# Attention and a mixture of experts in one kernel: the weight loads of experts 0, 1 and 2 are issued at other places

## The chip, the cores and the metric

The kernel runs on one core of a Trainium2 chip. The metric is the device time of one execution in microseconds (us). The core has five engines that work side by side, each through its own list of instructions in a fixed order: PE (TensorE, matrix products), ACT (ScalarE), DVE (VectorE), POOL (GpSimd) and SP (SyncE). They wait for one another, and for data transfers (DMAs), through semaphores. A DMA is issued by an engine, lands later, and its landing is what others wait for.

## The reference

Block-causal attention over 8 batches, 8 heads, 576 positions and 64 dimensions, and then a layer of 8 experts over its 4608 tokens of width 512; every token is given to two of the experts.

```python
# attention: q, k, v are 8 x 8 x 576 x 64
scores = scale * np.matmul(q, k.transpose(0, 1, 3, 2))
block_i = pos[:, None] // 64
block_j = pos[None, :] // 64
scores = np.where(block_i >= block_j, scores, -1000000000.0)
scores = scores - np.max(scores, axis=-1, keepdims=True)
attn = np.exp(scores)
attn = attn / (np.sum(attn, axis=-1, keepdims=True) + 1e-09)
attn_out = np.matmul(attn, v)

# experts: x is 4608 x 512, w1 is 8 x 512 x 1024, w2 is 8 x 1024 x 512
logits = x @ w_gate
noisy_logits = logits + np.log1p(np.exp(x @ w_noise)) * noise
top2 = np.argpartition(-noisy_logits, 2, axis=1)[:, :2]
# top2_w: softmax over the two chosen logits
for e in range(E):
    for k in range(2):
        mask = top2[:, k] == e
        h = np.maximum(x[mask] @ w1[e], 0.0)
        out[mask] += top2_w[mask, k, None] * (h @ w2[e])
```

## The kernel before

**Attention.** The batches are worked through in four groups of two (g = 0 to 3). A group has 26 score slots, two half groups of 13, and the slots are counted through: slot u = 26 g + place, 0 to 103. In every slot the main loop issues one score unit: PE's score matmuls (L297, L308) into the PSUM tile `sc`, and ACT's exponential of it into `esc` (L300, and L311 in the last slot of a half group). Behind the score unit come the steps that the program has put at that slot with `at(slot, function, arguments)`; `run(slot)` issues them, in an order of rank where several stand at one slot. The loads of weights and the scatters have the last rank, and among themselves the order in which they were put. The whole order of every engine is thus written out by hand: nothing is reordered later, and what an engine does waits for what stands before it in its own list.

The steps of a group g, apart from its score units:

- `load_all` (L206) brings raw q and k of group g+2, `load_v` (L210) the v tiles `vt` of group g+1, 16 small loads each. `transpose_qk` (L254) turns raw q and k on PE.
- `av_tile` (L339, L350) multiplies the exponentials by v; DVE divides by the sum (L354 for the reciprocal, L355 for the product) and writes the result as rows of `xr`, one tile of tokens after another. At a group's first tile POOL clears and fills some columns of the new `xr` (L327, L328). There are three `xr` buffers, so that group 3's waits for the scatters of group 0.
- `x_transpose` (L369, L370) and `router` (L382 to L469: PE, ACT and DVE in small steps) choose each token's two experts and its row in their lists.
- `scatter` (L489) writes rows of `xr` to a buffer in DRAM, `xd`, ordered by expert. It is an indirect DMA that POOL issues, 18 per group, with the row numbers from the router. It waits for an exponential of one or two slots before.

The scatters of group 0 stand at slots 52 to 69, of group 1 at 78 to 95, of group 2 at 101 to 114 and of group 3 at 118 to 131. Slots from 104 on have no score unit; from 111 on every slot is a step of the experts.

**Experts.** Groups 0 and 1 are one half of the tokens, groups 2 and 3 the other. For each half and expert, in the order (0,0), (0,1), (0,2), (1,0), (1,1), (1,2), (0,3), (1,3) and on, `load_x` brings that expert's rows, transposed, from `xd` (SP, L509, `xa` for the first and `xg` for the others; the first waits for all scatters of its half); `layer1` (L564 on PE, L567 on ACT) has eight steps and `layer2` (L576 on PE, L581 on ACT, L586 on DVE) five. Results of a token's first expert go to DRAM (`yd`, L583), are gathered for its second (L604, POOL), and the sum is scattered to the output (L588, POOL).

**Weights.** `load_w(pool, e, k)` (its DMA is L230) brings a quarter of expert e's weights: k = 0 and 1 are halves of `w1sb`, k = 2 and 3 halves of `w2sb`, 512 KB each in the buffer. The source is float32 and the buffer bfloat16; the DMA converts, and POOL issues it. Pool `wE` has room for two experts, 0 and 1. Pool `wM`, for expert 2, is opened at slot 91, when the raw q and k are no longer used. Later experts come during the expert steps.

**POOL's queue** therefore holds, in one order: raw q and k, v, weights, scatters, gathers and the output's scatters. A DMA that POOL issues waits for the eighth one before it on that queue to have landed, since eight semaphores are used in turn.

In the lines below `UG` is 26.

Of the kernel before, what the change touches and what calls it, by code (L numbers as in the profile page):

```python
# [19 lines left out]
def kernel(  # L20
# [43 lines left out]
    UG = 2 * UN  # L64
# [32 lines left out]
    wE = main.enter_context(tc.tile_pool(name="wE", bufs=2))  # L97
# [524 lines left out]
    def at(slot, fn, *args):  # L622
        todo.setdefault(slot, []).append((fn, args))

    def run(slot):

        def rank(item):
            fn, args = item
            if fn is router_step:
                return 3 if rgen_n.get(args[0], 0) in (0, 1, 2, 8, 14, 15) else 0  # L630
            return {av_tile: 1, transpose_qk: 2, x_transpose: 2}.get(fn, 4)

        items = todo.pop(slot, [])
        while items:
            items.sort(key=rank)
            fn, args = items.pop(0)
            fn(*args)
# [131 lines left out]
    at(UG + 4, clear_x, 0, UG + 3)  # L769
    at(2 * UG + 4, clear_x, 1, 2 * UG + 3)  # L770
    for k in range(4):
        at(UG + 1 + 2 * k, load_w, wE, 0, k)
        at(2 * UG - 6 + k, load_w, wE, 1, k)
    for u in range(NG * UG):
        score_unit(*divmod(u, UG))
        run(u)
        if u == 3 * UG + 13:
            raws_up.close()
            ffn["x"] = raws_up.enter_context(tc.tile_pool(name="xgp", bufs=3, side="right", reuse_waits="tile"))
            ffn["rec"] = raws_up.enter_context(tc.tile_pool(name="recp", bufs=1, side="right", reuse_waits="tile"))  # L780
            wM = raws_up.enter_context(tc.tile_pool(name="wM", bufs=1, side="right", reuse_waits="tile"))
            at(3 * UG + 18, load_x, 0)
            at(3 * UG + 19, load_x, 1)
            at(3 * UG + 20, load_rec, 0)
            at(3 * UG + 21, load_x, 2)
            for k in range(4):
                at(4 * UG + 12 + 3 * k, load_w, wM, 2, k)

    WL = {}

# [141 lines left out]
```

## Time and profile before

| | us |
|---|---|
| seven runs, sorted | 489.25, 490.5, 492.11, 496.56, 496.75, 497.06, 497.95 |
| their median | 496.56 |
| the profiled run's own time | 489.71 |
| its span (first to last instruction) | 487.8 |

Every time that follows is of that one profiled execution, in us from the start of its span. The busy times of the page, as shares of the span:

| engine | busy us | share |
|---|---|---|
| PE | 413.0 | 85% |
| ACT | 253.7 | 52% |
| POOL | 245.9 | 50% |
| DVE | 162.4 | 33% |

The span falls into these parts, by the last exponential of each half group and the first and last matmul of the experts:

| part | from | to |
|---|---|---|
| groups 0 and 1 (slots 0 to 51) | 0 | 75 |
| group 2, first half (slots 52 to 64) | 75 | 92 |
| group 2, second half (65 to 77) | 92 | 114 |
| group 3, first half (78 to 90) | 114 | 132 |
| group 3, second half (91 to 103) | 132 | 167 |
| rest of group 3, its transposes and router (104 to 110) | 167 | 194 |
| matmuls of the experts | 194 | 448 |
| last gathers and scatters of the output | 448 | 488 |

On POOL, the loads of expert 0 are issued at 46.1 to 49, those of expert 1 at 80.5 to 90.7, those of expert 2 at 201.5 to 219.3. The first scatter of group 0 is issued at 92.75, the last of group 1 at 154.78; those of group 2 run from 166.3 to 183.9, those of group 3 from 196.7 to 231.9.

How to read a line of the profile. A line of the timeline has the start, the duration, the engine and the source line, the operation, what it writes and reads, and in brackets the idle time of that engine before it, with what ended it: another engine's instruction, a DMA, "issue" when the engine waited for nothing that the profile shows, "remote" when a semaphore that no instruction in the trace explains came last. "PEclk" is the clock that was granted to PE, as a share of the full one. "DMA share" is the sum over queues of the time that packets took, as a share of the core's 16 DMA engines; since packets of one engine overlap, it can pass 1. The chain of waits is followed back from the last instruction: at each step to what released it.

### The profile page before, as it was taken

The page shows a single profiled execution, that of the slowest core. Times are in us where ns is not written, and L with a number is a line of the kernel's source. Part 1 is how long each engine was busy: PE and PEld are TensorE (multiplying, and loading weights), DVE is VectorE, ACT ScalarE, POOL GpSimd, SP SyncE. Part 2 cuts the span into 40 slices and gives each one's busy share as a digit, 9 for nine tenths or more (in the row PEclk, how much of TensorE's full clock was granted, in tenths as well). Part 3 has the DMA queues.
Part 4 walks back from the last instruction along what each step waited for, and adds up shares of the span by engine and source line. Part 5 has one row for each costly group of instructions (what it writes and reads, how often), then busy time and mean ns, then how long its engine had stood idle before and what let it go on. Part 6 is the DMA issues. An engine that isn't in the chain of part 4 may idle for free.

```text
span 487.8 us, 9833 instructions
## 1 busy us (share of the span) xinstructions
PE 413.0 (85%) x3952; PEld 255.0 (52%) x3952; DVE 162.4 (33%) x508; ACT 253.7 (52%) x343; POOL 245.9 (50%) x293
## 2 busy tenths in 40 slices
PE   3889879878930717997999999999989999999994
PEld 2456556655620416653655655665555664565562
DVE  1677678666640704820030011011011112113112
ACT  2999878866830500553545544554544554554340
POOL 8778225248876270587240123353537465565533
PEclk9989988975965755998999999999999999999998
DMA  9999999997932940488998668798899999864222
GB/s 143 158 142 177 229 208 182 223 232 106 119 112 89 159 146 24 99 183 212 136 222 179 97 154 184 131 213 194 141 225 198 183 237 240 168 187 166 76 80 97
DMA packets 134569, 78.67 MB, mean 161 GB/s; under 512 B 95937, under 2 KB 124355, under 8 KB 134516
## 3 DMA queue, kind: packets, MB, share of 16 engines
q0 software_dynamic: 70304, 55.78, 69.0%
q1 hardware_dynamic: 54132, 13.00, 15.1%
q10 hardware_dynamic: 10080, 9.18, 5.8%
q8 instruction: 33, 0.54, 0.5%
q14 instruction: 20, 0.16, 0.1%
HBM read 68.28 MB, written 33.13 MB: 208 GB/s over the span
## 4 chain that ended last, share of the span: by engine, by line
PE 66%; DMA 8%; ACT 6%; issue 6%; another core or an unknown queue 6%; DVE 3%; POOL 3%; POOLq 0%; DVEq 0%
PE yp L576 24%; PE hp L564 23%; PE av L339 6%; DMA raw<-in_k_dram 5%; PE sc L297 5%; ACT esc L300 4%; PE tp L254 3%; PE av L350 2%; PE tp L369 2%; POOL out_dram L588 2%; DMA yg<-yd,orow 1%; DMA yd<-ysb 1%; ACT hq L267 1%; DVE xr L355 1%
## 5 line engine op out<-in xcount | busy, mean ns | idle before, releaser
L576 PE MATMUL yp<-w2sb,hq 128*128 128x512 bf16 x640 | 142.7, 382 | 4.3 <-issue 2.6
L564 PE MATMUL hp<-xg,w1sb 128*128 128x320 bf16 x960 | 133.7, 299 | 1.9 <-ACT hq L567 1.3
L564 PEld LDWEIGHTS <-w1sb 128*128 128x128 bf16 x1024 | 100.1, 98 | 44.1 <-issue 3.1
L567 ACT ACTIVATE hq<-hp 128x640 bf16<-128x640 f32 x128 | 89.7, 703 | 60.3 <-PE hp L564 53.7
L586 DVE SCALAR_TENSOR_TENSOR yo<-yp,wrow,yg 128x512 f32<-128x512 f32 x46 | 34.5, 751 | 234.3 <-ACT ysb L581 183.2
L300 ACT ACTIVATE esc<-sc 128x1024 bf16<-128x1024 f32 x96 | 94.7, 1026 | 32.6 <-remote 18.9
L576 PEld LDWEIGHTS <-hq 128*128 128x128 bf16 x640 | 63.0, 98 | 78.8 <-issue 7.1
L489 POOL DMA_INDIRECT xd<-xr,slots x72 | 70.7, 982 | 55.4 <-issue 14.3
L604 POOL DMA_INDIRECT yg<-yd,orow x46 | 47.4, 1031 | 86.2 <-ACT hq L567 62.6
L581 ACT ACTIVATE ysb<-yp,wrow 128x512 bf16<-128x512 f32 x70 | 48.1, 687 | 79.9 <-PE yp L576 64.1
L588 POOL DMA_INDIRECT out_dram<-yo,trow x46 | 45.7, 994 | 58.1 <-DVE yo L586 48.1
L339 PE MATMUL av<-vt,esc 128*128 128x65 bf16 x640 | 35.6, 213 | 32.8 <-DVE xr L355 16.2
L339 PEld LDWEIGHTS <-esc 128*128 128x128 bf16 x640 | 27.8, 110 | 48.3 <-DVE xr L355 22.4
L297 PE MATMUL sc<-hq 64*128 64x512 bf16 (+4 forms) x320 | 42.5, 335 | 10.2 <-ACT esc L300 8.7
L210 POOL DMA_DIRECT2D vt<-in_v_dram x40 | 34.5, 875 | 20.1 <-DMA raw<-in_k_dram 5.6
L355 DVE TENSOR_TENSOR xr<-av,rden 128x256 bf16<-128x256 f32 x72 | 30.5, 424 | 2.7
L254 PE MATMUL tp<-ident,raw 128*64 128x128 bf16 x512 | 24.3, 247 | 6.7 <-DMA raw<-in_k_dram 3.7
L354 DVE RECIPROCAL rden<-av 128x4 f32<-128x4 f32 x72 | 13.3, 184 | 43.9 <-remote 28.7
L267 ACT ACTIVATE hq<-tp 128x1024 bf16<-128x1024 bf16 (+1 forms) x20 | 17.1, 853 | 16.3 <-PE tp L254 7.1
L254 PEld LDWEIGHTS <-raw 128*64 128x64 bf16 x512 | 18.6, 125 | 11.5 <-DMA raw<-in_k_dram 4.1
L297 PEld LDWEIGHTS <-hq 64*128 64x128 bf16 x320 | 12.4, 97 | 19.3 <-issue 11.4
L260 DVE COPY hq<-tp 128x1024 bf16<-128x1024 bf16 (+1 forms) x24 | 14.4, 598 | 8.8 <-PE tp L254 4.5
(122 smaller groups left out, 229.5 us busy)
## 6 DMA issues: line engine op xcount, KB each, us to landing
yd<-ysb ACTq DMA_DIRECT2D x70, 128.0 KB
w1sb<-in_moe_w_dram POOLq DMA_DIRECT2D x16, 512.0 KB
w2sb<-in_moe_w_dram POOLq DMA_DIRECT2D x16, 512.0 KB
vt<-in_v_dram POOLq DMA_DIRECT2D x32, 128.0 KB
raw<-in_q_dram POOLq DMA_DIRECT2D x2, 1152.0 KB
raw<-in_k_dram POOLq DMA_DIRECT2D x2, 1152.0 KB
xd<-zero SPq DMA_DIRECT2D x16, 132.0 KB
raw<-in_q_dram POOLq DMA_DIRECT2D x8, 256.0 KB
```

What stands on the lines that cost most here:

```text
L254: nc.tensor.transpose(to[64 * hf:64 * hf + 64, :, r, :], raw[:, (t0, t1)[hf], r * 64:(r + 1) * 64], ident)
L297: nc.tensor.matmul(out=sc[:, hf, off:off + z - a], lhsT=kT[sl, c0 + jt * P:c0 + jt * P + P], rhs=qT[sl, c0 + a:c0 + z], start=True, stop=True)
L300: ins = nc.scalar.activation(out=esc[:, hh, :, piece * 512:(piece + 1) * 512], in_=sc, func=AF.Exp, scale=scale)
L339: nc.tensor.matmul(out=av[:, hh, :], lhsT=esc[:, hh, hf, c:c + P], rhs=vb[:, 4 * hf + jt, h, :], start=(jt == 0), stop=(jt == ib))
L355: nc.vector.tensor_tensor(out=xr[:, idx, st * SET * D:(st + 1) * SET * D].rearrange("p (h d) -> p h d", h=SET), in0=av[:, :, 0:D], in1=rde ...
L489: ins = nc.gpsimd.indirect_dma_start(out=xd[half].bitcast(I32), out_offset=bass.IndirectOffsetOnAxis(ap=slots[:, g * TG + idx, i:i + 1], a ...
L564: nc.tensor.matmul(out=hp[:, n, 0:NW], lhsT=w1sb[:, db, fb * P:(fb + 1) * P], rhs=xgs[b][:, db, n * NW:(n + 1) * NW], start=(db == 0), sto ...
L567: ins = nc.scalar.activation(out=hs[b][:, fb, :].rearrange("p (n w) -> p n w", n=2), in_=hp[:, :, 0:NW], func=AF.Relu)
L576: nc.tensor.matmul(out=yp, lhsT=hs[b][:, fb, c * P:(c + 1) * P], rhs=w2sb[:, fb, :], start=(fb == 0), stop=(fb == FB - 1))
L581: ins = nc.scalar.activation(out=ysb, in_=yp, func=AF.Copy, scale=w)
L588: ins = nc.gpsimd.indirect_dma_start(out=out, out_offset=bass.IndirectOffsetOnAxis(ap=trow[half][:, e, c:c + 1], axis=0), in_=yo, in_offse ...
L604: ins = nc.gpsimd.indirect_dma_start(out=yg, out_offset=None, in_=yd[half][0:e * CAP, :], in_offset=bass.IndirectOffsetOnAxis(ap=orows[hal ...
```

## The change

Three numbers of slots change. Expert 0's four loads go from slots 27, 29, 31, 33 to 46, 47, 48, 49, where expert 1's were. Expert 1's go from there to slots 80, 84, 88, 92. Expert 2's go from slots 116, 119, 122, 125 to 112, 114, 117, 120.

```diff
     for k in range(4):
-        at(UG + 1 + 2 * k, load_w, wE, 0, k)
-        at(2 * UG - 6 + k, load_w, wE, 1, k)
+        at(2 * UG - 6 + k, load_w, wE, 0, k)
+        at(3 * UG + 2 + 4 * k, load_w, wE, 1, k)
     for u in range(NG * UG):
         score_unit(*divmod(u, UG))
         run(u)
@@
             for k in range(4):
-                at(4 * UG + 12 + 3 * k, load_w, wM, 2, k)
+                at(4 * UG + (8, 10, 13, 16)[k], load_w, wM, 2, k)
```

In POOL's queue this takes four loads out of the second group's stretch, puts expert 0's loads ahead of the first scatter of group 0, puts expert 1's among the scatters of group 1, one after the third, the seventh, the eleventh and the fifteenth, and lets the first load of expert 2 follow the fifteenth scatter of group 2. The other engines' orders are the same as before.

## The prediction

> **What bounds the kernel now.** I read the table of engine time by stretches first, cut at the ends of the half groups of 13 score slots (slot 65 begins near 92, 78 near 114, 91 near 132, 104 near 167).
>
> ```profile
> 75.00:92.00 17.00, 16.87 (x328) 12.15 (x329) 13.63 (x39) 13.48 (x16) 7.06 (x9) 0.90 1.76 207
> 92.00:114.00 22.00, 15.80 (x248) 10.27 (x248) 13.72 (x48) 15.21 (x22) 10.86 (x11) 0.74 0.99 199
> 114.00:132.00 18.00, 17.67 (x326) 12.42 (x326) 13.15 (x38) 13.27 (x16) 15.98 (x19) 0.85 1.11 120
> 132.00:167.00 35.00, 13.72 (x200) 8.41 (x198) 13.80 (x52) 13.69 (x20) 19.09 (x22) 0.61 0.51 113
> 167.00:194.00 27.00, 11.54 (x181) 9.71 (x182) 9.20 (x27) 0.67 (x2) 12.91 (x14) 0.57 0.40 97
> 194.00:448.00 254.00, 247.44 (x1487) 144.41 (x1485) 43.00 (x108) 127.65 (x188) 117.02 (x122) 0.99 0.83 178
> ```
>
> After the stretch and its length stand the busy times of PE, PE's weight loads, DVE, ACT and POOL, then PE's granted clock, DMA share and GB/s. From 194 on the experts keep PE at 247 of 254 us. The odd stretches are 132–167 and 167–194: no engine is busy for even 60% of them, and the DMA share is at its lowest. A half group elsewhere takes 17 to 22 us. The chain of waits names what ends last there:
>
> ```profile
> 45.13 19.55 DMA raw<-in_k_dram
> ...
> 141.96 10.70 another core or an unknown queue
> 153.32 5.22 another core or an unknown queue
> 169.72 2.38 another core or an unknown queue
> 172.77 7.87 another core or an unknown queue
> ```
>
> The timeline shows the middle of it:
>
> ```profile
> 151.83 0.21 POOL L328 COPY xr<-tokm 128x9 int32<-128x9 int32 x1
> 152.21 0.99 POOL L489 DMA_INDIRECT xd<-xr,slots  x1 [0.16 <-issue]
> 152.68 0.18 DVE L354 RECIPROCAL rden<-av 128x4 f32<-128x4 f32 x1 [10.72 <-remote]
> ...
> 154.78 0.97 POOL L489 DMA_INDIRECT xd<-xr,slots  x1 [0.30 <-issue]
> 157.61 1.02 ACT L300 ACTIVATE esc<-sc 128x1024 bf16<-128x1024 f32 x1 [13.82 <-remote]
> ```
>
> PE finished the av tile that L354 reads at 138.5 and the scores that L300 reads at 139.1, but its word of it reached DVE at 152.7 and ACT at 157.6; PE then stood for want of their buffers (10.3 us before 153.4, 5.5 before 159.3). All that time POOL issued the second group's scatters, each 0.97 us and 0.30 of issue, one directly behind the other. The word came just after two other instructions of POOL (L327, L328), and again after the last scatter (154.78). From 166.3 to 183.9 it repeats with the third group's 18 scatters (PE waits of 2.4, 8.1, 1.3 and 2.0). Where scatters alternate with v loads, 114–131, PE is busy 17.67 of 18. So I read 35 and 27 us as a half group of about 18 and a tail of about 14, drawn out by unbroken trains of scatters. What makes the signals late I cannot see.
>
> **The change part by part.** [...]No load is added.
>
> *Expert 0's four loads leave slots 27–33 for 46–49.* On POOL they cost 4 x 0.77 us (their own row). Behind them it is their transfers that count: they landed at 67.2, 69.6, 72.1 and 74.8, so 4 x 2.5 = 10 us of the queue, and the v loads behind waited for each:
>
> ```profile
> 59.37 0.87 POOL L210 DMA_DIRECT2D vt<-in_v_dram  x1 [5.00 <-DMA raw<-in_q_dram]
> 65.21 0.88 POOL L210 DMA_DIRECT2D vt<-in_v_dram  x1 [4.97 <-DMA raw<-in_k_dram]
> 67.43 0.87 POOL L210 DMA_DIRECT2D vt<-in_v_dram  x1 [1.34 <-DMA w1sb<-in_moe_w_dram]
> 69.88 0.88 POOL L210 DMA_DIRECT2D vt<-in_v_dram  x1 [1.58 <-DMA w1sb<-in_moe_w_dram]
> ...
> 92.75 1.09 POOL L489 DMA_INDIRECT xd<-xr,slots  x1 [1.36 <-DMA xd<-zero]
> ```
>
> Every transfer from POOL waits for the eighth before it. The raw q and k of the third group lie ahead of expert 0's loads, so PE's waits for them (1.55 us at 58.9, 2.56 at 64.7) stay: worth 0 here. What gains is POOL's backlog: expert 0's loads now take the place that expert 1's had, all behind comes some 10 us sooner, and the first group's scatters, placed at slots 52 to 69 (75 to 98) but begun at 92.75, can begin at about 82 and end near 120 instead of 131. PE's time hides all this (16.87 of 17 busy until 92), so by itself it gives 0; if the cover were gone, 10 us at most. Expert 0 is then in at about 95 and needed after 165.
>
> *Expert 1's loads leave 46–49 for 80, 84, 88, 92.* POOL's order for the second group becomes 3 scatters, load, 4, load, 4, load, 4, load, L327 and L328, 3 scatters. These must be costed together with the train they break. Its own time: 18 x 1.27 + 4 x (0.77 + 0.3) = 27 us instead of 23, begun at about 120 instead of 132.8, so ended at about 147 instead of 155.75. Each load's 2.5 us of transfer fills the queue that ran at 0.51 share. What the breaks do to PE is not shown by before for weight loads between scatters in attention. Bounds: nothing (all 20.2 us of PE waits in 133–159, 1.5 + 2.96 + 10.3 + 5.5, stay), or all go. The nearest row is 114–132 (one v load after each scatter: waits gone); the next is 92–114, with runs of two and three scatters (waits of 1.1, 1.3 and 2.0). Runs of four lie nearest the latter: I keep 4 us of 20.2 and take 16. PE's 13.7 us of work there ran at clock 0.61 and would shorten; ACT's 13.7 for 13 exps and copies then bounds the half group at about 18, so I add 1 only: **−17 us**.
>
> *A rule against this.* The Trainium skill, page "SBUF — State Buffer", section "Who interferes with whom", says "PE and ACT never wait on anyone" and that DMA does not contend with a compute engine. By that rule a train of scatters cannot be what delays PE, breaking it returns nothing, and the sum is 0 to −5 us (POOL's earlier end alone). The trace has 10.72 and 13.82 us of late words inside the train, and with v loads between the scatters PE has no wait over 1 us. I go by the trace, but the rule is a reason to leave the case of no gain standing.
>
> *Expert 2's loads move from 116, 119, 122, 125 to 112, 114, 117, 120.* On POOL: 15 of the third group's scatters run before the first, so that train is hardly broken. I keep the waits of 167–194: 0, with −10 as the other end (the train may also meet SP's transposes of x, 158–166 before). The loads, at 201.5 to 219.3 before, are needed only at expert 2's first layer (235.8): cover of 16 us, which grows. The first gather stands behind them on POOL; PE's wait of 2.61 us for it at 226.2 may go: −1, between −2.6 and +2.5 (a load's transfer).
>
> *Clock.* Windows show 0.61 and 0.57 from 132 to 194. The skill's "TensorE: Matmul & The Clock Gate", Part 1, says that idling halves the clock and about 4 us of steady work brings it back. By the rule a closed-up half group runs at full clock and 14 us of PE work becomes about 9, 5 us more than I count; by the trace even 114–132, nearly full, had 0.85 and 18 us. I take the trace.
>
> **Sum.** 0 − 17 + 0 − 1 = −18 against the profiled run's own 489.7 (span 487.8 and 1.9 around it): 472. The shown runs lie in two heaps, three at 489–492 and four at 496–498, median 496.56; the profiled one is of the lower. I don't know to which heap the new kernel's runs would belong and put 3 us on it: **475**.
>
> **Rivals.**
>
> *The stall belongs to the number of scatters, not to their lying together.* 36 scatters remain, the waits only move forward with the train. For it: the small waits at 100–113, where the train was not unbroken; the rule above. Against: 114–132, eight scatters, none. Time: 0 to −5, so 490 to 496 against the median, 493 in the middle.
>
> *The train's length sets the stall: slower.* PE's word stays late until the last scatter of the second group is through, as at 157.6. Then the loads in between only lengthen it: 4 x 1.07 = 4.3 us of POOL, and 10 if each transfer holds up the eighth behind it. If POOL's front gain is lost on the way (the scatters are tied to exps one or two slots back, so they cannot begin before 114, and stalls moved forward delay those exps too), the train ends at 160 to 166 instead of 155.75, and router, transposes and experts follow: +4 to +10, so 501 to 507 against the median, 504 in the middle. It decides from the point at which that train ends after 155.75. For it: weight loads are the longest transfers on that queue (2.5 us against 1.03 for a v load), and four of them come where POOL is already the busiest engine (19 of 35). Against: 10 us of earlier start outweigh 4.3.
>
> That a load comes too late for its expert would be another, but expert 1 is in by about 150 and needed at about 190: under 2 in 100, left in the above.
>
> **How the numbers follow.** Stall broken 0.62: 458 (third group's train too, −10, and full clock) to 484. Number of scatters 0.14. Length of train 0.24. A measurement of this kernel tells from no change what differs by more than about 1%, 5 us: below 491.6 or above 501.5. Faster: all of the first and 0.04 of the second, 0.66. Same: 0.10 of the second and 0.05 of the third, 0.15. Slower: 0.19 of the third. A range of 458 to 503 leaves out about 2 in 10, half of the slower case among it. The likeliest case's own range is 462 to 484.
>
> **What would show it.** Right: the exps of the third group's second half take about 18 us instead of 35; the two long waits "remote" before L354 and L300 (10.7, 13.8) gone; the second group's last scatter at about 147; clock over 0.8 there; first expert matmul at about 176. Wrong: the waits stand as long, beside scatters with loads between; or that last scatter comes after 155.75. Third train: if its waits go as well, 8.1 and the small ones, I have been too careful.

## The result, and the profile after

| | before | after |
|---|---|---|
| median of all runs taken for the comparison | 491.83 us (63 runs) | 486.69 us (26 runs) |
| ratio after to before, with its 95% interval | | 0.985 [0.982, 0.989] |
| the profiled run's own time | 489.71 us | 490.76 us |

The ratio and its interval compare only the runs within 1.5% of each kernel's fastest one, so 0.985 is not the quotient of the two medians, which lie 5.1 us apart.

The change makes the kernel 1.5% faster, some 7.3 us of 492. The sign was forecast and the size was not: 475 against 496.56 was a gain of 4.3%, and 486.69 lies outside the likeliest case's own range of 462 to 484. The profiled run of the kernel after happened to be one of its longer ones, 4 us above its median, while the one before was 2 us below its own. So the spans do not show the gain; what the stretches show of it is told below.

The table of stretches of the kernel after, cut at the ends of its half groups (92.7, 112.8, 139.8, 160.4). The columns are start and end, length, busy times of PE, PE's weight loads, DVE, ACT and POOL, PE's granted clock, DMA share, GB/s:

```profile
92.00:112.00 20.00, 15.13 (x256) 10.24 (x255) 13.50 (x47) 14.84 (x21) 13.47 (x14) 0.83 0.90 161
112.00:130.00 18.00, 15.77 (x268) 10.64 (x267) 11.60 (x36) 11.29 (x14) 15.10 (x19) 0.86 0.90 119
130.00:160.00 30.00, 19.10 (x268) 11.97 (x266) 16.25 (x57) 16.73 (x23) 15.93 (x19) 0.57 0.79 154
160.00:188.00 28.00, 11.32 (x195) 9.48 (x192) 9.10 (x27) 0.93 (x6) 12.70 (x14) 0.63 0.54 111
```

The stretch 130 to 160 is still at clock 0.57 with no engine over two thirds busy. The last half group of attention did shrink as forecast, from 35.0 to 20.6 us, but the half group before it grew from 18.6 to 27.0. Both together went from 53.6 to 47.6: 6 us, not 17.

The chain of waits shows the same. Behind the start in us stand the length and what was waited for:

```profile
44.27 19.34 DMA raw<-in_k_dram
...
123.36 2.28 another core or an unknown queue
...
162.65 3.63 another core or an unknown queue
166.94 7.42 issue
175.00 4.24 another core or an unknown queue
```

The waits of 10.70 and 5.22 us at 142 and 153 are gone. In their place stand smaller ones from 123 on, where the second group's train now begins (a "train" is a group's run of scatters on POOL). ACT's timeline has them one by one, some named remote, others ended by PE itself; the bracket is the idle time ahead of an exponential and what ended it:

```profile
125.72 1.02 ACT L300 ACTIVATE esc<-sc 128x1024 bf16<-128x1024 f32 x1 [2.08 <-remote]
...
131.17 1.02 ACT L300 ACTIVATE esc<-sc 128x1024 bf16<-128x1024 f32 x1 [2.82 <-PE sc L297]
...
135.69 1.02 ACT L300 ACTIVATE esc<-sc 128x1024 bf16<-128x1024 f32 x1 [1.97 <-PE sc L297]
139.39 0.38 ACT L311 ACTIVATE esc<-sc 128x256 bf16<-128x256 f32 x1 [2.68 <-PE tp L254]
```

On POOL the first group's first scatter and the second group's last are these:

```profile
79.60 1.09 POOL L489 DMA_INDIRECT xd<-xr,slots  x1 [1.11 <-DVE hq L265]
...
149.70 0.97 POOL L489 DMA_INDIRECT xd<-xr,slots  x1 [0.30 <-issue]
```

The first is 13.2 us sooner than before (92.75). Of this, 10.6 are left at the first group's last scatter (130.0 to 119.4), and then the train of the second group takes 27.5 us instead of 22.0. So its end comes 5.1 us sooner, 149.7 against 154.8; the last exponential follows 7.3 us sooner (167.7 to 160.4) and the first expert matmul 7.6 (194.3 to 186.7). The stretch between the last exponential and that matmul did not change (26.6 and 26.3):

```profile
194.31 0.98 PE L564 MATMUL hp<-xa,w1sb 128*128 128x320 bf16 x5
```

```profile
186.69 1.52 PE L564 MATMUL hp<-xa,w1sb 128*128 128x320 bf16 x10
```

These 7.6 us are about the measured gain, but this one profile loses them again: from that matmul to the end it takes 302.2 us, before 293.5. That part comes back at the end of the experiments.

So two readings stand against each other. The prediction's: loads between scatters break the train, and so give PE's word way. The other, which takes over the place (not the sign) of the third case of the prediction: it is the end of the second group's train that sets the start of the experts, the gain is that the train starts sooner, and the loads inside it give nothing.

### The profile page after: what moved, and what is told of

Read it like the earlier page. It is cut to its first block, busy times and chain, and to the rows that moved or that the text cites. A ratio compares the mean times of both kernels' runs of the same rounds, so it can differ in the third digit from the quotient of the medians.

```text
span 488.9 us, 9834 instructions
## 1 busy us (share of the span) xinstructions
PE 418.4 (86%) x3952; PEld 257.4 (53%) x3952; DVE 161.7 (33%) x508; ACT 253.2 (52%) x343; POOL 246.5 (50%) x293
## 3 DMA queue, kind: packets, MB, share of 16 engines
q1 hardware_dynamic: 54132, 13.00, 16.1%
## 4 chain that ended last, share of the span: by engine, by line
PE 61%; DMA 10%; issue 8%; DVE 8%; ACT 7%; POOL 3%; another core or an unknown queue 2%; POOLq 0%; ACTq 0%; DVEq 0%
PE hp L564 23%; PE yp L576 23%; DMA raw<-in_k_dram 5%; PE sc L297 4%; ACT esc L300 4%; PE av L339 4%; DMA yd<-ysb 3%; PE tp L254 3%; DVE xr L355 2%; POOL out_dram L588 2%; DMA yg<-yd,orow 2%; PE av L350 1%; ACT hq L267 1%; PE tp L369 1%
## 5 line engine op out<-in xcount | busy, mean ns | idle before, releaser
L564 PE MATMUL hp<-xg,w1sb 128*128 128x320 bf16 x960 | 137.6, 304 | 8.4 <-ACT hq L567 8.4
L564 PEld LDWEIGHTS <-w1sb 128*128 128x128 bf16 x1024 | 101.5, 99 | 52.7 <-issue 9.3
L300 ACT ACTIVATE esc<-sc 128x1024 bf16<-128x1024 f32 x96 | 94.0, 1025 | 19.9 <-PE sc L297 16.1
L254 PE MATMUL tp<-ident,raw 128*64 128x128 bf16 x512 | 26.0, 256 | 6.7 <-issue 3.1
L267 ACT ACTIVATE hq<-tp 128x1024 bf16<-128x1024 bf16 (+1 forms) x20 | 17.0, 852 | 18.1 <-PE tp L254 5.1
L254 PEld LDWEIGHTS <-raw 128*64 128x64 bf16 x512 | 20.0, 131 | 11.8 <-issue 6.6
L354 DVE RECIPROCAL rden<-av 128x4 f32<-128x4 f32 x72 | 13.4, 185 | 28.4 <-remote 8.5
L260 DVE COPY hq<-tp 128x1024 bf16<-128x1024 bf16 (+1 forms) x24 | 14.7, 612 | 11.5 <-PE tp L254 5.2
```

What stands on the lines that cost most here:

```text
L254: nc.tensor.transpose(to[64 * hf:64 * hf + 64, :, r, :], raw[:, (t0, t1)[hf], r * 64:(r + 1) * 64], ident)
L300: ins = nc.scalar.activation(out=esc[:, hh, :, piece * 512:(piece + 1) * 512], in_=sc, func=AF.Exp, scale=scale)
L564: nc.tensor.matmul(out=hp[:, n, 0:NW], lhsT=w1sb[:, db, fb * P:(fb + 1) * P], rhs=xgs[b][:, db, n * NW:(n + 1) * NW], start=(db == 0), sto ...
```

## Experiments

Ratios are against the kernel before, timed beside each kernel on the same chip. They were timed at five times (each part below is one, the last is two), under two conditions. At the first and the fourth time the kernel before took 496 and 493 us (the slower condition, in which the result was measured too), in the others 467 to 471 (the quicker one).

### Which part of the change gives the gain

`e01_only`: expert 2's loads stay.

```diff
-                at(4 * UG + (8, 10, 13, 16)[k], load_w, wM, 2, k)
+                at(4 * UG + 12 + 3 * k, load_w, wM, 2, k)
```

> The change without its third line: expert 2's loads stay at slots 116, 119, 122, 125. If the whole effect lies in the loads of experts 0 and 1 (scatters of the first and second group begun earlier, the second group's train broken by loads), the ratio is that of the whole change, 0.985, within half a per cent. If the move of expert 2's loads gave part of it, or took part of it back, the ratio differs from 0.985 by more than that.

`no_breaks`, in addition: expert 1's loads behind the train.

```diff
-        at(3 * UG + 2 + 4 * k, load_w, wE, 1, k)
+        at(3 * UG + 18 + k, load_w, wE, 1, k)
```

> Experts 0's loads at 46 to 49 as after the change, but expert 1's all four behind the last scatter of the second group (slots 96 to 99), expert 2's as before the change. The same four loads are gone from ahead of the first group's scatters; only the loads between the scatters are missing. If the loads between the scatters are what shortened the third group's second half (35.0 to 20.6 us), this half and the one before it are 50 us or more together again, and the ratio is 0.995 or more. If the earlier start of the scatters is what counts, and the breaks only lengthen the train, the ratio is 0.985 or less, and the two halves take 47 us or less together.

`memset_breaks`, on the kernel before:

```diff
         scat[half].append(ins.ins.name)
+        if g in (1, 2):
+            nc.gpsimd.memset(scr, 0.0)
```

> The kernel before, with one small POOL memset of a scratch tile behind each of the 36 scatters of the second and third group; nothing is moved. If any other instruction between two scatters lets the delayed word of PE through, the halves of the third group take some 18 us each, the waits named remote before L354 and L300 (10.7 and 13.8 us) vanish, and the ratio is 0.96 to 0.975. If the delay belongs to the number of scatters or to their transfers, the waits stay, and the ratio is 1.00 to 1.01, from 36 x 0.1 to 0.2 us more on POOL.

`e2_only`, on the kernel before:

```diff
-                at(4 * UG + 12 + 3 * k, load_w, wM, 2, k)
+                at(4 * UG + (8, 10, 13, 16)[k], load_w, wM, 2, k)
```

> The third line alone: only expert 2's loads move, to 112, 114, 117, 120. Fifteen scatters of the third group still lie ahead of the first of them. If only unbroken scatters delay the word of PE, the stretch from the last exponential to the first expert matmul stays at 26 to 27 us and the ratio is 0.995 to 1.003. If a load on POOL's queue beside the end of attention costs PE time, it is over 1.005.

| | ratio | last scatter of group 1 | last exponential | first expert matmul | both halves of group 3 |
|---|---|---|---|---|---|
| before | | 154.8 | 167.7 | 194.3 | 53.6 |
| after | 0.985 [0.982, 0.989] | 149.7 | 160.4 | 186.7 | 47.6 |
| `e01_only` | 0.990 [0.985, 0.994] | 151.8 | 162.6 | 188.8 | 47.9 |
| `no_breaks` | 0.985 [0.980, 0.990] | 152.1 | 163.6 | 190.6 | 47.9 |
| `memset_breaks` | 0.997 [0.993, 1.001] | 158.7 | 170.1 | 197.5 | 54.3 |
| `e2_only` | 1.015 [1.008, 1.022] | 158.6 | 170.0 | 196.3 | 54.2 |

`e01_only` is within half a per cent of the whole change, as expected if expert 2's move gives nothing. `no_breaks` decides about the breaks. With no load in the train the whole gain is there, and group 3 takes 47.9 us as in `e01_only` (0.9 us over the limit that was set for this outcome, 2.1 under that of the other). So the breaks are worth nothing measurable.

`memset_breaks` agrees in its time, but fits neither of its two cases. The two long waits named remote before L354 and L300 are not there, and yet the two halves take 54.3 us: PE's lost time stands elsewhere, as in this line.

```profile
146.28 0.38 ACT L311 ACTIVATE esc<-sc 128x256 bf16<-128x256 f32 x1 [11.29 <-PE sc L297]
```

In `e2_only`, whose order up to slot 111 is that of the kernel before, they stand elsewhere again (6.85 us before L267 at 147.1). Which instruction a late word meets therefore changes from one execution to the next, and that two waits of one profile are gone in another proves little by itself.

In all six rows the last exponential comes 10.7 to 12.9 us behind the issue of the last scatter, and the first expert matmul 37.0 to 39.5. This is weaker than it looks. A scatter waits for an exponential of one or two slots before, and in every row but the first it did so inside the train, for 2 to 7 us in all. Seven or eight exponentials are left behind the last scatter, and these alone take 7.3 and 10.4 us in `after_again` below, where nothing is late. In `no_breaks` the train without loads took 29.3 us, longer than the 27.5 with them:

```profile
131.85 0.97 POOL L489 DMA_INDIRECT xd<-xr,slots  x1 [0.31 <-issue]
135.88 0.97 POOL L489 DMA_INDIRECT xd<-xr,slots  x1 [3.07 <-ACT esc L300]
138.57 0.97 POOL L489 DMA_INDIRECT xd<-xr,slots  x1 [1.71 <-ACT esc L300]
...
152.09 0.98 POOL L489 DMA_INDIRECT xd<-xr,slots  x1 [0.30 <-issue]
```

So in this condition the train and the exponentials hold each other up, and which of them leads is not shown. Nor does a run exclude that such pauses act as breaks of their own; the loads, at any rate, are not needed for the gain. What is shown is that scatters begun earlier go with experts begun earlier, with or without breaks.

`e2_only` came out at 1.015, over the 1.005 set for the case that the move costs PE time. But the stretch from the last exponential to the first expert matmul, where the cost was looked for, stayed at 26.3 us. It comes back below.

### The same chain where PE's word is not late

`after_again`, `e01_again` and `e2_again` are repeats. `late_g2`, on the kernel after, puts the third group's train beside the expert steps:

```diff
-            at(r0 + r1 + (j if g < 2 else 4 * j // 5), scatter, g, j)
+            at(r0 + r1 + (j if g < 2 else 10 + j // 2 if g == 2 else 4 * j // 5), scatter, g, j)
```

> The changed kernel once more, for a second profile and beside the two halves of the change on one chip. In the six profiles at hand the third group's last half (of group index 3) ends 10.7 to 12.9 us behind the issue of the second group's last scatter, and the experts start 37 to 39.5 us behind it. If that train sets the end of attention, this holds again, with a ratio of 0.985. If the two were only late together by chance, the distance differs by more than 3 us.

> The change without the move of expert 2's loads, beside the whole change. If expert 2's move is neutral, its ratio is within half a per cent of that of the whole change; if the move costs what it seemed to cost alone (1.5%), this one is faster by 1% or more.

> Expert 2's move alone, again: up to slot 111 every engine's order is that of the kernel before, yet it measured 1.015 in four runs. If the loads beside the third group's scatters cost time, it is over 1.008 again; if those few runs drew a long attention stretch by chance, it is 0.997 to 1.006.

> The changed kernel with the third group's 18 scatters taken out of the tail of attention (slots 101 to 114) and put beside the first expert steps (111 to 119). Nothing but POOL's order changes. If scatters on POOL are what delays PE's word in the tail, the stretch from the last exponential to the first expert matmul falls from 26 to about 15 us, and the ratio is 0.96 to 0.97. If the tail is bound by its own chain (av tiles, transposes, router), it stays at 24 us or more and the ratio is 0.985, or above it where the later scatters delay the second half's rows.

The kernel before took 28 us less here, the repeated kernels 30 to 37. The stretches of `after_again` (columns as above) show where:

```profile
91.00:107.00 16.00, 13.37 (x232) 8.87 (x230) 13.29 (x48) 14.70 (x21) 9.24 (x10) 0.89 0.86 177
107.00:124.00 17.00, 16.12 (x348) 11.88 (x350) 13.62 (x39) 13.78 (x17) 14.72 (x18) 1.00 1.07 121
124.00:140.00 16.00, 13.15 (x178) 7.77 (x179) 12.70 (x48) 12.83 (x18) 12.65 (x15) 0.68 0.75 159
140.00:157.00 17.00, 9.11 (x187) 7.93 (x186) 12.54 (x37) 0.96 (x5) 13.48 (x16) 0.78 0.89 198
```

Each half group takes 16 to 17 us, beside the same scatters, and no wait named remote is listed between 90 and 157. The late words are therefore not what a train always does. By its own test `after_again` missed: the last exponential does not follow the last scatter by 10.7 to 12.9 us, it comes 6.8 us before it. Yet the ratio is 0.980 [0.973, 0.986], no smaller a gain. The expert's first matmul names what holds it here:

```profile
147.27 0.97 POOL L489 DMA_INDIRECT xd<-xr,slots  x1 [0.30 <-issue]
...
157.15 3.10 PE L564 MATMUL hp<-xa,w1sb 128*128 128x320 bf16 x12 [6.11 <-DMA xa<-xd]
```

PE is done with attention at 151.0 and stands 6.1 us for `xa`. SP issues that transpose at 151.33, when all scatters of the half have landed, the last of which POOL issued at 147.3. So in this condition the end of the second group's train sets the start of the experts, by a plain dependency, about 10 us behind it instead of 37. `e2_again`, whose order up to there is that of the kernel before, shows much the same distance, its last scatter 7.4 us and its first expert matmul 6.4 us later:

```profile
154.71 0.97 POOL L489 DMA_INDIRECT xd<-xr,slots  x1 [0.30 <-issue]
...
163.57 0.72 PE L564 MATMUL hp<-xa,w1sb 128*128 128x320 bf16 x2 [6.72 <-DMA xa<-xd]
```

The earlier first train also removes a wait here that the order before has. DVE's first write into group 3's `xr` stood 4.50 us, and PE 4.51 us for it. The profile names no releaser for it ("issue"). But by the program that write may go ahead only when group 0's scatters have landed, since they read the same buffer, and the last of them was issued at 129.7 (119.1 in `after_again`, which has no such wait). The start of the experts hides it, as PE waits 6.72 us for `xa` anyway.

```profile
133.41 0.42 DVE L355 TENSOR_TENSOR xr<-av,rden 128x256 bf16<-128x256 f32 x1 [4.50 <-issue]
```

`e01_again` gave 0.979 [0.974, 0.983], as the whole change. `e2_again` gave 0.991 [0.987, 0.996], the other side of its first result. `late_g2` missed, 0.997 [0.993, 1.000]: in this condition there is nothing in the tail to gain (15.5 us from last exponential to first expert matmul, 16.7 in `after_again`), and the first gather of the experts now stands behind more scatters on POOL. PE waited 10.75 us for it, 3.35 in `after_again`:

```profile
203.49 1.87 PE L576 MATMUL yp<-w2sb,hq 128*128 128x512 bf16 x4 [10.75 <-DVE yo L586]
```

Whether a later third train would pay where the words are late was not tried.

### Six more scatters, and other places for the loads

`six_more`, on the kernel after: six copies of one scatter in the middle of the second group's train.

```diff
         scat[half].append(ins.ins.name)
+        if (g, j) == (1, 8):
+            for t in range(6):
+                nc.gpsimd.indirect_dma_start(
+                    out=xs[t].bitcast(I32), out_offset=bass.IndirectOffsetOnAxis(
+                        ap=slots[:, g * TG + idx, i:i + 1], axis=0),
...
```

> The changed kernel with six more scatters in the middle of the second group's train, copies of one real scatter written to six buffers that nobody reads. PE, ACT, DVE and SP have the same orders. If the end of that train sets the start of the experts, everything from there moves by 6 x 1.27 = 7.6 us: the last scatter, the first expert matmul, and the time, to a ratio of 0.995 to 1.003 against before. If the train is covered by PE's and ACT's own work, the ratio stays at that of the change, within half a per cent.

`e1_late`, on the kernel before:

```diff
-        at(2 * UG - 6 + k, load_w, wE, 1, k)
+        at(3 * UG + 18 + k, load_w, wE, 1, k)
```

> One line of the kernel before: expert 1's loads at 96 to 99, behind the second group's train, instead of 46 to 49; experts 0 and 2 stay where they were. If all that matters is how many loads stand on POOL directly ahead of the first group's scatters (four instead of eight), its ratio is that of the change, 0.98 to 0.986. If expert 0's early place (10 us of the ring in 64 to 75) is what held POOL up, the scatters begin as late as before and the ratio is 0.995 or more.

`best1`, on the kernel after (with expert 2 as before):

```diff
-        at(3 * UG + 2 + 4 * k, load_w, wE, 1, k)
+        at(2 * UG + 2 + 2 * k, load_w, wE, 1, k)
```

> Expert 0's loads at 46 to 49 as after the change, expert 1's at 54, 56, 58, 60, among the first group's early scatters, where POOL stood idle for 10 to 15 us in all waiting for exponentials; expert 2's as before the change. No load lies in the second group's train. If POOL's queue from the first scatter to the last of the second group sets the start of the experts, that last scatter is issued 3 to 5 us sooner than after the change, the experts start as much sooner, and the ratio to before is 0.970 to 0.978. If the loads' transfers in the ring hold the scatters up instead, the train ends as late as before and the ratio is 0.99 or more.

> The changed kernel on the same chip as these three, for the comparison and for a third profile: 0.98 to 0.986 against before. Where the chip is one on which PE's word comes promptly (a half group takes 16 to 17 us), the first expert matmul waits for the transposed rows, about 10 us behind the last scatter; where it comes late, it starts about 37 us behind it.

| | ratio | last scatter of group 1 | first expert matmul | SP's issuing of `xa` |
|---|---|---|---|---|
| `after_third` | 0.985 [0.978, 0.991] | 150.9 | 162.4 | 4.00 |
| `six_more` | 1.001 [0.997, 1.005] | 156.1 | 166.7 | 2.71 |
| `e1_late` | 0.995 [0.992, 0.999] | 145.3 | 166.2 | 12.98 |
| `best1` | 0.989 [0.983, 0.995] | 150.8 | 160.5 | 3.63 |

`six_more` hits in its time. Six scatters of 1.27 us took the gain away whole: 1.65% of 467 is 7.7 us (the intervals allow 3 to 4 us either way), and 7.6 were expected. The train itself grew from 25.3 to 33.0 us, which is 7.7 again. In these two profiles it began 2.5 us sooner with the six, so its last scatter comes 5.2 us later and the first expert matmul 4.3, not 7.6. PE's wait for `xa` grew to 12.95 us, against 7.22 in `after_third`:

```profile
166.73 1.52 PE L572 MATMUL hp<-xa,w1sb 128*128 128x320 bf16 x5 [12.95 <-DMA xa<-xd]
```

```profile
162.42 2.05 PE L564 MATMUL hp<-xa,w1sb 128*128 128x320 bf16 x7 [7.22 <-DMA xa<-xd]
```

(The lines of `six_more` are numbered eight further on there.) In both, the experts begin 10.6 and 11.5 us behind the last scatter, when `xa` has landed. So in this condition the train's length is paid for.

`e1_late` shows why the loads should nevertheless not stand right behind the train. Its scatters begin at 81.0 and it has the earliest last scatter of all, 145.3. So expert 0's early place costs POOL nothing: what counts is that four loads instead of eight stand ahead of the first scatter. But the experts start 21 us behind the last one, and the ratio is only 0.995. SP's queue in `e1_late`, the start of each transpose and how long SP took to issue it:

```profile
148.17 12.98 SPq L509 DMA_TRANSPOSE xa<-xd  x1
161.25 5.08 SPq L509 DMA_TRANSPOSE xg<-xd  x1
```

and in `after_again`:

```profile
151.33 2.70 SPq L509 DMA_TRANSPOSE xa<-xd  x1
154.14 3.44 SPq L509 DMA_TRANSPOSE xg<-xd  x1
```

The landing comes later than the end of the issuing: `xa` landed 18.0 us behind its start in `e1_late` and 5.8 in `after_again`. While expert 1's loads lasted, up to 162, the transposes' packets and the loads' came one for one (304 of 256 bytes and 304 on the loads' queue, nearly all of 1 KB, between 154 and 156; 302 and 307 between 160 and 162). Without the loads, `after_again` moved 1759 packets of transposes between 154 and 156. Inside the train the loads lengthen it by 3.4 us (25.3 us in `after_again`, 22.0 in `e1_late`); behind it, they cost 12.2 us of `xa`. Where the words are late this is hidden: in `no_breaks` SP took 11.82 us to issue `xa`, and nothing was lost by it.

`best1` missed its first case and came near its second (0.99 or more). The loads hold the scatters up where they follow each other in POOL's ring: POOL waited up to 3.64 us for landings there, and the train ended at 150.8, no sooner than after the change.

### Once more, and expert 2

`before_again`, `after_fourth`, and `e1_tail`, on the kernel after:

```diff
-        at(3 * UG + 2 + 4 * k, load_w, wE, 1, k)
+        at(4 * UG + 1 + k, load_w, wE, 1, k)
```

> The kernel before, once more, for a profile beside two others on one chip. If PE's late word belongs to the train of scatters, the third group's second half (index 3) takes some 35 us and the waits remote before L354 and L300 are over 10 us wherever the train is unbroken. If it belongs to the chip or the execution, a chip that runs the kernel in about 468 us shows 17 us and no such wait, and the experts wait for xa, about 9 us behind the last scatter, instead. The ratio is 0.995 to 1.005 either way.

> The changed kernel with expert 1's four loads at slots 105 to 108, among the third group's scatters, instead of in the second group's train. If the loads in the train cost their POOL time (4.3 us), the second group's last scatter and the transpose of xa come 3 to 4.5 us sooner than after the change, and the ratio is 0.972 to 0.979. If the loads' transfers lie beside the transposes and slow them, as they did right behind the train (12.98 us for xa instead of 2.70), the gain is given back and the ratio is 0.985 to 0.995.

> The changed kernel beside these two: 0.98 to 0.986. Its second group's last scatter is issued 5 to 7 us before that of the kernel before, and the first expert matmul starts as much sooner.

These kernels met the slower condition. `before_again` (ratio 1.001) repeats the stretch that the prediction read, the second half of group 3 at 36.9 us. Its waits named remote there are of 3.6 to 6.6 us, though, not over 10.

```profile
110.00:130.00 20.00, 18.25 (x352) 13.00 (x347) 13.69 (x39) 13.55 (x17) 17.36 (x20) 0.91 0.91 111
130.00:166.00 36.00, 14.86 (x175) 8.49 (x171) 13.02 (x48) 13.20 (x18) 22.20 (x26) 0.53 0.53 121
```

It has its last scatter at 155.6 and its first expert matmul at 193.3. `after_fourth` has 151.4 and 189.5, `e1_tail` 149.9 and 185.0, so the experts again begin earlier where the train ends earlier. Over the profiles of this condition the two orders keep apart: the three with the order before up to slot 111 have their last scatter at 154.8, 155.6 and 158.7, the two of the kernel after at 149.7 and 151.4.

But the times hardly show it: 0.997 [0.990, 1.004] and 0.995 [0.988, 1.002]. `after_fourth` missed, and does not confirm the 0.985 of the result: the intervals do not meet. `e1_tail` comes near the ratio of its second case without the reason, as SP issued `xa` in 2.54 us. From the first expert matmul to the end the two took 305.5 and 311.5 us, the kernel before 293.9. In that part ACT had stood 11.0 and 16.1 us for the landing of results on their way to `yd`. Of the profiles in this condition, the four with expert 2's move took 302 to 312 us there, the five without it 293 to 296. This is not yet a cost of the move: all four are of runs longer than their kernel's median, and all five of runs shorter than theirs, so a long run alone could explain it. Three more kernels were run for that move:

> The change without expert 2's move, beside the whole change and beside that move alone, on one chip. From the first expert matmul to the end it took 293 to 296 us in the profiles of such kernels. If the move costs time there, this kernel is faster than the whole change by 1% or more; if it is neutral, they agree within half a per cent.

> Expert 2's move alone, a third time. It measured 1.015 on a chip with late words of PE and 0.991 on one without. If it costs time in the expert steps on the former, the ratio is 1.008 or more there, with 302 us or more from the first expert matmul to the end; if neutral, 0.995 to 1.005.

> The changed kernel beside these two. If expert 2's move gives part of the gain back, it stands at 0.99 to 1.00, with 302 us or more from the first expert matmul to the end; if the move is neutral, at 0.980 to 0.986, as the kernel without it.

They met the quicker condition: `e01_third` 0.984 [0.974, 0.993], `e2_third` 0.989 [0.983, 0.995], `after_fifth` 0.977 [0.970, 0.985]. There the move alone gives about 1% (twice, where nothing or a loss was expected), and with the rest no difference that the intervals tell. In the slower condition it cost 1.5% alone in four runs, and was not run there beside `e01_only` and the whole change. Whether it gives a part of the gain back there stays open, and so does why results land later in `yd` then.

No kernel tried is shown to be faster than the kernel after: `e01_again` equals it, the others are slower or within the intervals.

## Why the prediction was wrong

**POOL's earlier start: right in size.** The scatters were to begin at about 82 and the first group's to end near 120; they began at 79.6 and ended at 119.4. The waits for raw q and k stayed. The train was to last 27 us and its last scatter to come at about 147: 27.5, and 149.7. The reason holds only in part. The prediction took the 10 us from expert 0's transfers at 64 to 75, but in `e1_late` expert 0's loads stay there and the scatters begin at 81.0 all the same. Which four of the eight loads go makes no difference. And 27.5 is in part a coincidence, as the train without loads took 29.3 in this condition.

**The step that failed** is in "Expert 1's loads leave 46–49 for 80, 84, 88, 92": of 20.2 us of PE waits I kept 4 and took 16, because loads would break the train, and so put −17 into the sum. Measured, both halves of group 3 gave 6.0 us, and `no_breaks` gave 5.7 of these with no break at all. The second half became 14.4 us shorter, but the first half, into which the train had moved, took 8.4 us more. I had costed one stretch and not asked what the moved train would do where it now lies. The row I leaned on, 114–132 with v loads between scatters, was weak evidence for breaks: beside an unbroken train in the quicker condition (`e1_late`) the two halves of group 3 take 33.8 us together, as smooth as any. What makes PE's words late in the slower condition, and whether the train or the exponentials lead there, stays open. Nothing points to late loading of instructions: between 134 and 160, around the waits of 10.72 and 13.82 us, the profile before has no packet on the queues that carry them.

**The tail at 0: right** (26.6 to 26.3). **Expert 2's move at −1:** not settled, as told above.

**The rivals.** The one that held the number of scatters to be what counts gave 0 to −5, and lies nearest to the −7.3 measured. The one that held the train's length to be what counts named the right place and rule, "it decides from the point at which that train ends after 155.75", and `six_more` shows that rule at work in the quicker condition, where the reason is the wait for `xa` and not a late word. Only the train ended at 149.7. A case that put both together, late words until the last scatter and that scatter 5 to 9 us sooner, would have come nearest and had no number of its own.

**The rule of the skill that spoke against me,** that PE never waits on anyone, gave a sum of 0 to −5 us. I read too much into it: it speaks of engines that contend for ports of SBUF, and the slower condition shows words that arrive late (10.7 and 13.8 us, and 31.0 us in six waits before L354 in `before_again`), not an engine held at a port. So no run here tests the rule. The measured gain is nearer to the sum by the rule than to mine, but not for its reason. **The clock** did not return: 0.57 between 130 and 160, as waits remained. In the quicker condition, without them, it was 1.00 in the first half of group 3 and 0.68 in the second (`after_again`), so a closed-up half does not always run at full clock either.

## What to carry to other kernels

Where an engine's queue runs without a pause from one point of the program to the next, a step on it is priced by when the queue's last needed item comes out, here the scatter that frees the first transpose. In the quicker condition six more items of 1.27 us made the train 7.7 us longer and took the gain away. A wait that seems to belong to the stretch in which it is seen moves with its cause: cost the stretch into which the cause is moved as well. And before a theory is built on waits that no dependency explains, look whether they are there at all in a second profile.

## What the runs showed of the hardware

Two conditions of the same kernel lie 25 us apart: about 468 and about 493 us. In the slower, DVE and ACT stood up to 12.2 us (`memset_breaks`) and 13.8 us (before) for words of PE, in waits that the profile calls remote. In the eleven profiles of the quicker no such wait of over 1.5 us was found between 90 and 195, beside the same trains of scatters. Whether it is the chip, or what else ran at the time, no run here tells. The first and the third part of the experiments bear the same chip number (7) and met different conditions; if the number names one chip, it is not the chip.

Transposing DMAs beside weight loads on another queue slow down: `xa` landed after 18.0 us (`e1_late`) instead of 5.8 (`after_again`), and SP's issuing of it took 12.98 us instead of 2.70. The packet counts, one for one, agree with what the Trainium skill says in "DMA: Bandwidth & Descriptors", section "Queues, rings and completion order": that an engine goes round between the queues that have work, packet by packet. With packets of 256 bytes against 1 KB, the transposes then got about a fifth of the bytes.
